# A whole filter loaded up front, weight transfers on another queue, and the last weight conversions moved into the first quads

## The chip, the cores and the metric

The kernel runs on one core of one Trainium2 chip. The metric is the device time in microseconds (us), the median of several executions. "Span" is the profiled execution from first to last instruction. It was 2769.5 us for the kernel before.

## The reference

```python
X = np.fft.rfft(x, axis=1)                      # x: (8, 3008, 256) fp32
Y = X * (filt_r + 1j * filt_i)[None, :, :]      # filter: (1505, 256), two parts
y = np.fft.irfft(Y, n=3008, axis=1)
h = y.reshape(24064, 256) @ w_in                # w_in  (256, 2048), float64 in memory
g = np.where(h > 0, h, np.exp(np.minimum(h, 0)) - 1)
out = g @ w_out                                 # w_out (2048, 256), float64 in memory
```

So there is a filter along the sequence for each of eight batches, and then a two-layer network over all tokens. The network's weights arrive as float64. The kernel reads them as pairs of 32-bit words and builds fp32 values from the bits, in 16 pieces ("weight 0" to "weight 15").

## The kernel before

Each batch is transformed in stages. Stage A multiplies chunks of x by a table (TensorE), copies the result out (ScalarE) and writes it to DRAM as z. Stage B reads z back in eight groups of frequencies, transforms each group, multiplies it by the filter (`b_unit`, four products on VectorE, two adds on GpSimd), transforms back (`bi_unit`) and writes y to DRAM. The layer then runs in quads of an up step and a down step. For batch 0 nothing of the layer can run beside stages A and B, so they are a serial prologue. Later batches' stages are spread into the layer's quads.

The prologue is what the change edits, together with a few things that hang on it:

```python
FBUFS = 3                                  # filter groups held at once
LO, HI = slice(0, 48), slice(64, 112)      # the partitions that hold filter and z

def f_read_first(g):                       # one group of the filter
    t = fbufs[g % FBUFS]
    for c, src in enumerate((filt_r, filt_i)):
        queue = nc.sync if c and g >= FBUFS else nc.gpsimd
        for a in range(2):
            r = a * 64
            k2 = 4 * g + 2 * a
            queue.dma_start(t[r:r + 24, c, :, :], raw(src, k2, [[64 * D, 24], [1, 2 * D]]))
            u = 1 if k2 == 0 else 0
            for r0, n in ((24, 16), (40, 7)):       # the mirrored half, read backwards
                queue.dma_start(t[r + r0:r + r0 + n, c, u:2, :],
                                raw(src, 64 * (r0 - 23) - k2 - u, [[64 * D, n], [-D, 2 - u], [1, D]]))
...
def w_fetch(k):                            # 512 KB of float64 weights into one of 3 places
    ...
        nc.scalar.dma_start(wd[:, ts(i, n), :].rearrange("p a w -> p (a w)"), s)

def w_convert(k):                          # VectorE: 3 tensor_scalars and 3 two-input steps,
    ...                                    # 4 adds more for odd k; ScalarE: 3 activations
    nc.scalar.activation(out=e, in_=e, func=AXT.Copy, scale=2.0 ** 23, bias=-896.0 * 2.0 ** 23)
    ...
# the prologue
for c in range(NXC):                       # stage A, six chunks
    a_unit(0, c); ...; z_write(0, c)
    w_fetch(2 + c)
    w_convert(c)
    if c == 1:
        for g in range(FBUFS):
            f_read_first(g)                # 3 of 8 groups
...
for g in range(NG + 2):                    # stage B, eight groups
    ...
        b_unit(0, g)
    ...
    if g + FBUFS < NG:
        f_read_first(g + FBUFS)
    if g < 8:
        w_fetch(8 + g)
    if g > 0:
        w_convert(6 + g)                   # a conversion in nearly every group
```

In the down step of every fourth quad stands one add on GpSimd, `nc.gpsimd.tensor_tensor(out=p3, in0=p3, in1=k[0][:, 1, 0:h], op=ALU.add)`. In quad 3 GpSimd also issues a rearrangement of the filter (`f_arrange`) for the later batches.

## Time and profile before

| | us |
|---|---|
| median of the runs of before beside the result (4 runs) | 2768.46 |
| first filter product on VectorE (end of stage A) | 55.24 |
| first matmul of the layer (end of stage B and its round trip) | 136.02 |
| first up step of quad 4 | 185.17 |
| first matmul of the next normalising step, behind the stop at 206 us | 225.92 |
| TensorE busy, of 2769.5 us | 2671.7 (96%) |

The prologue takes 136 us, 5% of the time. These five marks cut the span into pieces, and each was read from the timeline. This is how the first looks in VectorE's timeline of the kernel before (start, length, engine, line, operation, output and inputs with shapes; in brackets the idle time ahead and what ended it):

```profile
55.24 0.69 DVE L226 TENSOR_TENSOR sr<-psr,f 128x512 f32<-128x512 f32 x1 [3.00 <-PE psi L215]
```

In TensorE's waits over the whole span (waiting line, releaser, total us, times, longest), the prologue's transfers and the stop at 206 us stand out:

```profile
PE psr L215 <- DMA t<-z: 17.7, 2, 13.3
PE psn L269 <- DMA t<-yd: 13.4, 1, 13.4
PE pso L427 <- DVE g L320: 11.8, 1, 11.8
...
PE psa L171 <- DMA xc<-in_x_dram: 11.0, 3, 5.5
PE phc L315 <- DVE si L227: 5.8, 14, 0.7
```

### The profile page before, as it was taken

The numbers are of one execution on the slowest core, as the hardware profiler recorded it, in microseconds if no ns is written. First come the engines' busy times: TensorE is split into PE (matmuls) and PEld (weight loads), VectorE is DVE, ScalarE is ACT, GpSimd is POOL, SyncE is SP. The second block draws the span as 40 slices with busy tenths as digits, with TensorE's granted clock in tenths as the row PEclk, the third lists the DMA queues.
The fourth block names the chain that finished last, engine by engine and source line by source line (L and its number), as shares of the span: only waits on it lengthen the run. The fifth ranks groups of instructions, "written<-read, shape, count | busy, mean of one in ns | idle before, by whom it ended". The sixth has DMA issues, their size and how long they took to land.

```text
span 2769.5 us, 36728 instructions
## 1 busy us (share of the span) xinstructions
PE 2671.7 (96%) x13376; PEld 2282.2 (82%) x13376; DVE 1999.9 (72%) x3363; ACT 1339.6 (48%) x2297; POOL 314.1 (11%) x393
## 2 busy tenths in 40 slices
PE   4598999999999999999999999999999999999999
PEld 2197778987899878998789877898789987899887
DVE  5865877677776777767866687767777677777776
ACT  3344444544455445554455544455444544554544
POOL 4321210002000120001200021000210012000000
PEclk7599999999999999999999999999999999999999
DMA  8563321343114331243312332133321233110010
GB/s 241 159 158 97 92 63 37 101 103 94 48 39 108 89 94 37 56 119 77 82 50 76 98 84 71 37 100 98 91 57 39 78 75 94 37 39 19 22 25 16
DMA packets 144366, 214.53 MB, mean 77 GB/s; under 512 B 26368, under 2 KB 100620, under 8 KB 144186
## 3 DMA queue, kind: packets, MB, share of 16 engines
q1 hardware_dynamic: 123706, 174.57, 24.2%
q0 software_dynamic: 16160, 27.65, 4.1%
q10 hardware_dynamic: 4320, 9.96, 1.2%
q8 instruction: 106, 1.74, 0.3%
q14 instruction: 74, 0.61, 0.1%
HBM read 137.04 MB, written 78.12 MB: 78 GB/s over the span
## 4 chain that ended last, share of the span: by engine, by line
PE 85%; DVE 6%; DMA 4%; ACT 3%; issue 1%; POOL 1%; SPq 0%; DVEq 0%; ACTq 0%; POOLq 0%
PE po L388 37%; PE pha L315 11%; PE phc L315 11%; PE phd L315 11%; PE phb L315 5%; PE psa L171 3%; PE psn L269 2%; PE pso L427 2%; PE psr L215 1%; PE pva L215 1%; DVE g L320 1%; ACT e L327 1%; ACT e L326 1%; DVE c L406 1%; DVE g L331 1%
## 5 line engine op out<-in xcount | busy, mean ns | idle before, releaser
L388 PE MATMUL po<-g,wo 128*128 128x256 f32 (+1 forms) x5376 | 1324.3, 375 | 0.0
L388 PEld LDWEIGHTS po<-g,wo 128*128 128x128 f32 x5376 | 1021.4, 190 | 116.3
L326 ACT ACTIVATE e<-g 128x512 f32<-128x512 f32 (+1 forms) x576 | 357.4, 621 | 619.7 <-DVE g L320 619.5
L327 ACT ACTIVATE e<-e 128x512 f32<-128x512 f32 (+1 forms) x768 | 477.5, 622 | 24.3
L320 DVE TENSOR_TENSOR g<-phc,g 128x512 f32<-128x512 f32 (+1 forms) x384 | 259.3, 675 | 227.2 <-PE phc L315 227.2
L331 DVE SCALAR_TENSOR_TENSOR g<-e,g 128x512 f32<-128x512 f32 (+1 forms) x576 | 387.2, 672 | 14.5 <-ACT e L327 13.8
L315 PE MATMUL pha<-y,wi 128*128 128x256 f32 (+1 forms) x1536 | 395.6, 380 | 0.1
L326 ACT ACTIVATE e<-pha 128x512 f32<-128x512 f32 (+1 forms) x192 | 112.9, 588 | 530.1 <-PE pha L315 527.2
L315 PEld LDWEIGHTS pha<-y,wi 128*128 128x128 f32 x1536 | 285.0, 190 | 83.5 <-ACT t L241 34.1
L320 DVE TENSOR_TENSOR g<-phd,g 128x512 f32<-128x512 f32 (+1 forms) x384 | 261.0, 680 | 85.9 <-PE phd L315 65.7
L331 DVE SCALAR_TENSOR_TENSOR g<-e,pha 128x512 f32<-128x512 f32 (+1 forms) x192 | 129.2, 673 | 258.9 <-ACT e L327 258.9
L315 PE MATMUL phc<-ys,wi 128*128 128x256 f32 (+1 forms) x768 | 194.7, 376 | 5.8 <-DVE si L227 5.8
L395 POOL TENSOR_TENSOR k<-k,k 128x256 f32<-128x256 f32 (+1 forms) x48 | 34.5, 719 | 1457.4 <-ACT k L392 1417.9
L315 PE MATMUL phd<-y,wi 128*128 128x256 f32 (+1 forms) x768 | 194.7, 376 | 1.3
L315 PE MATMUL phc<-y,wi 128*128 128x256 f32 (+1 forms) x768 | 194.8, 376 | 0.0
L315 PE MATMUL phb<-ys,wi 128*128 128x256 f32 (+1 forms) x768 | 193.9, 375 | 0.0
L315 PE MATMUL phd<-ys,wi 128*128 128x256 f32 (+1 forms) x768 | 193.8, 375 | 0.0
L315 PEld LDWEIGHTS phc<-ys,wi 128*128 128x128 f32 x768 | 144.7, 190 | 26.8 <-issue 11.0
L315 PEld LDWEIGHTS phd<-y,wi 128*128 128x128 f32 x768 | 144.7, 190 | 22.3 <-PE phc L315 6.5
L335 ACT ACTIVATE g<-pha 128x512 f32<-128x512 f32 (+1 forms) x192 | 112.6, 586 | 103.6 <-PE pha L315 103.5
L230 POOL TENSOR_TENSOR sr<-sr,sp 128x512 f32<-128x512 f32 x64 | 81.2, 1268 | 698.3 <-DVE sp L228 698.3
L315 PEld LDWEIGHTS phb<-ys,wi 128*128 128x128 f32 x768 | 145.9, 190 | 17.0 <-issue 0.5
(92 smaller groups left out, 2939.5 us busy)
## 6 DMA issues: line engine op xcount, KB each, us to landing
z<-t SPq DMA_DIRECT2D x192, 128.0 KB
t<-z SPq DMA_DIRECT2D x128, 192.0 KB
yd<-t SPq DMA_DIRECT2D x128, 192.0 KB
t<-yd SPq DMA_DIRECT2D x192, 128.0 KB
xc<-in_x_dram SPq DMA_DIRECT2D x88, 256.0 KB
out_dram<-o SPq DMA_DIRECT2D x176, 128.0 KB
f<-fd POOLq DMA_DIRECT2D x112, 192.0 KB, 3.5
tn<-tn_t SPq DMA_DIRECT2D x48, 256.0 KB
```

What stands on the lines that cost most here:

```text
L171: nc.tensor.matmul(ps[:, u, :], w[:, r + u, :], xt[:, r + u, :], start=True, stop=True)
L215: nc.tensor.matmul(ps[:, u:u + w, :], table[k, v, :], rhs[k, u:u + w, :], start=True, stop=True)
L230: nc.gpsimd.tensor_tensor(out=sr, in0=sr, in1=p, op=ALU.subtract)
L269: nc.tensor.matmul(ps[:, ts(q, P)], t[:, i - 4 * m, ds(dh * P, P)], w[:, i - 4 * m, :], start=True, stop=True)
L315: nc.tensor.matmul(banks[key][:, a, 0:h], w_in[q][:, COMBO[n], a, :], y[n], start=start and a == 0, stop=True, skip_group_check=True)
L320: nc.vector.tensor_tensor(out=g[o], in0=i0, in1=i1, op=ALU.add)
L326: nc.scalar.activation(out=e, in_=src, func=AXT.Relu, scale=-1.0)
L327: nc.scalar.activation(out=e, in_=e, func=AXT.Exp, scale=-1.0)
L331: nc.vector.scalar_tensor_tensor(out=g[n], in0=es[n], scalar=1.0, in1=src, op0=ALU.subtract, op1=ALU.max)
L335: nc.scalar.activation(out=g["t1"], in_=mm(1, "a", True), func=AXT.Copy)
L388: nc.tensor.matmul(po[i][:, u, 0:h], w_out[q][:, COMBO[n], a, :], g[n][:, a, :], start=q == 0 and a == 0 and n in (1, 3, 6, 4), stop=True, ...
L427: nc.tensor.transpose(ps[0:w, u, ts(dh, P)], c[dh][:, ds((2 * a + u) * P, w)], eye)
```

## The change

The intent is to empty stage B. There VectorE converts a weight in almost every group, and SyncE and ScalarE queue small filter transfers and weight transfers among those of z and y. So the whole filter of batch 0 goes into one place of 32 KB per partition, which buffers of the layer take over later. The weights go to GpSimd's queue and land in the old filter buffers. Stage B keeps only every other conversion, and weights 12 to 15 are converted beside the layer's first quads. One step of each conversion goes from ScalarE to VectorE, and so does the add of the down step, from GpSimd.

```diff
-    def f_read_first(g):
+    def f_read_first(t):                   # all eight groups at once, 22 transfers
...
-                queue.dma_start(t[r:r + 24, c, :, :], raw(src, k2, [[64 * D, 24], [1, 2 * D]]))
+                nc.gpsimd.dma_start(t[r:r + 24, :, c, :, :].rearrange("q g u d -> q g (u d)"),
+                                    raw(src, 2 * a, [[64 * D, 24], [4 * D, NG], [1, 2 * D]]))
...
-                    nc.gpsimd.tensor_tensor(out=p3, in0=p3, in1=k[0][:, 1, 0:h], op=ALU.add)
+                    nc.vector.tensor_tensor(out=p3, in0=p3, in1=k[0][:, 1, 0:h], op=ALU.add)
...
-            nc.scalar.dma_start(wd[:, ts(i, n), :].rearrange("p a w -> p (a w)"), s)
+            nc.gpsimd.dma_start(wd[:, ts(i, n), :].rearrange("p a w -> p (a w)"), s)
...
-        nc.scalar.activation(out=e, in_=e, func=AXT.Copy, scale=2.0 ** 23, bias=-896.0 * 2.0 ** 23)
+        nc.vector.tensor_scalar(out=e, in0=e, scalar1=896.0, scalar2=8388608.0,
+                                op0=ALU.subtract, op1=ALU.mult)
...
+            w_fetch(2)
+            f_read_first(ff)               # ahead of weight 3 in GpSimd's queue
+            for c in range(NXC):
+                a_unit(0, c)
...
+                w_convert(c)
+                w_fetch(3 + c)
...
+                    b_unit(0, g, ff[:, g])
...
+                if g % 2 == 1:
+                    k = 6 + g // 2
+                    w_convert(k)
+                    w_fetch(k + 3)
...
+        w_convert(11)
+        w_fetch(14)
...
+        for k in range(12, 16):
+            at((0, 0, 1, 2)[k - 12], 1, w_convert, k)
```

More of the change, by code (lines that the diff above doesn't have):

```diff
@@ L125 @@
     t4p = pool("t4p", 2)
-    yp = pool("yp", 2)
-    gp = pool("gp", 2)
-    ep = pool("ep", 2)
     kp = pool("kp", 1)
-    op = pool("op", 1)
     zp = pool("zp", 2, space=DRAM)
@@ L193, in f_read @@
             nc.gpsimd.dma_start(t[r].rearrange("p c u d -> p (c u d)"), fd[g, a].rearrange("q c u d -> q (c u d)"))
-    def f_read_first(g):
-        t = fbufs[g % FBUFS]
+    def f_read_first(t):
         for c, src in enumerate((filt_r, filt_i)):
-            queue = nc.sync if c and g >= FBUFS else nc.gpsimd
             for a in range(2):
                 r = a * 64
-                k2 = 4 * g + 2 * a
-                queue.dma_start(t[r:r + 24, c, :, :], raw(src, k2, [[64 * D, 24], [1, 2 * D]]))
-                u = 1 if k2 == 0 else 0
-                for r0, n in ((24, 16), (40, 7)):
-                    queue.dma_start(t[r + r0:r + r0 + n, c, u:2, :],
-                                        raw(src, 64 * (r0 - 23) - k2 - u, [[64 * D, n], [-D, 2 - u], [1, D]]))
-            if g == 0:
-                queue.dma_start(t[24:48, c, 0, :], raw(src, 32, [[64 * D, 24], [1, D]]))
+                nc.gpsimd.dma_start(t[r:r + 24, :, c, :, :].rearrange("q g u d -> q g (u d)"),
+                                    raw(src, 2 * a, [[64 * D, 24], [4 * D, NG], [1, 2 * D]]))
+                for u in range(2):
+                    g0 = 1 if a == u == 0 else 0
+                    for r0, n in ((24, 16), (40, 7)):
+                        nc.gpsimd.dma_start(t[r + r0:r + r0 + n, g0:NG, c, u, :],
+                                            raw(src, 64 * (r0 - 23) - 4 * g0 - 2 * a - u,
+                                                [[64 * D, n], [-4 * D, NG - g0], [1, D]]))
+            nc.gpsimd.dma_start(t[24:48, 0, c, 0, :], raw(src, 32, [[64 * D, 24], [1, D]]))
     def tile_mm(ps, table, k, rhs, special):
@@ L215, in tile_mm, with b_unit @@
             nc.tensor.matmul(ps[:, u:u + w, :], table[k, v, :], rhs[k, u:u + w, :], start=True, stop=True)
-    def b_unit(b, g):
-        t, f = t2s.pop((b, g)), fbufs[(b * NG + g) % FBUFS]
+    def b_unit(b, g, f=None):
+        t = t2s.pop((b, g))
+        f = fbufs[(b * NG + g) % FBUFS] if f is None else f
         re, im = (psM.tile([P, 2, D], FP32, tag="mx", name=n) for n in ("psr", "psi"))
@@ L446, in w_fetch @@
         q, j = divmod(k, 4)
-        wd = wds[k] = gp.tile([P, 512, 2], U32, tag="g%d" % (1 + k % 3), name="wd")
+        wd = wds[k] = fbufs[k % FBUFS].bitcast(U32).rearrange("p c u d -> p (c u d)").rearrange("p (a w) -> p a w", w=2)
         if j < 2:
@@ L515 @@
     with tc.manual_schedule():
-        for c in range(XBUFS):
-            x_load(0, c, nc.scalar)
-        for f in fbufs:
-            nc.vector.memset(f, 0.0)
-        for k in range(2):
-            w_fetch(k)
-        nc.gpsimd.tensor_copy(out=junk[0:1], in_=xs[0, 1][0:1, 0, 0:1])
-        for t, d in ((gb, gb_d), (gr, gr_d), (gi, gi_d), (eye, id_d)):
-            nc.gpsimd.dma_start(t, d)
-        for c in range(NXC):
-            a_unit(0, c)
-            if c + XBUFS < NXC:
-                x_load(0, c + XBUFS, nc.scalar)
-            z_write(0, c)
-            w_fetch(2 + c)
-            w_convert(c)
-            if c == 1:
-                for g in range(FBUFS):
-                    f_read_first(g)
@@ L536 @@
-        z_read(0, 0)
-        z_read(0, 1)
-        w_convert(6)
-        for g in range(NG + 2):
-            if g >= 2:
-                bi_unit(0, g - 2)
-            if g < NG:
-                b_unit(0, g)
-                if g + 2 < NG:
-                    z_read(0, g + 2)
-            if g >= 2:
-                y_write(0, g - 2)
-            if g + FBUFS < NG:
-                f_read_first(g + FBUFS)
-            if g < 8:
-                w_fetch(8 + g)
-            if g > 0:
-                w_convert(6 + g)
+        with tc.tile_pool(name="boot", bufs=1) as bp:
+            ff = bp.tile([P, NG, 2, 2, D], FP32, name="ff")
+            for k in range(2):
+                w_fetch(k)
+            for c in range(XBUFS):
+                x_load(0, c, nc.scalar)
+            nc.vector.memset(ff, 0.0)
+            nc.gpsimd.tensor_copy(out=junk[0:1], in_=xs[0, 2][0:1, 0, 0:1])
+            for t, d in ((gb, gb_d), (gr, gr_d), (gi, gi_d)):
+                nc.gpsimd.dma_start(t, d)
+            w_fetch(2)
+            f_read_first(ff)
+            for c in range(NXC):
+                a_unit(0, c)
+                if c + XBUFS < NXC:
+                    x_load(0, c + XBUFS, nc.scalar)
+                z_write(0, c)
+                w_convert(c)
+                w_fetch(3 + c)
+            z_read(0, 0)
+            z_read(0, 1)
+            for g in range(NG + 2):
+                if g >= 2:
+                    bi_unit(0, g - 2)
+                if g < NG:
+                    b_unit(0, g, ff[:, g])
+                    if g + 2 < NG:
+                        z_read(0, g + 2)
+                if g >= 2:
+                    y_write(0, g - 2)
+                if g % 2 == 1:
+                    k = 6 + g // 2
+                    w_convert(k)
+                    w_fetch(k + 3)
@@ L554 @@
+        yp = pool("yp", 2)
+        gp = pool("gp", 2)
+        ep = pool("ep", 2)
+        op = pool("op", 1)
         y_read(0, 0)
+        w_convert(11)
+        w_fetch(14)
+        nc.scalar.dma_start(eye, id_d)
         n_unit(0, 0)
@@ L567 @@
             at(c - 1, 0, x_load, 1, c)
+        for k in range(12, 16):
+            at((0, 0, 1, 2)[k - 12], 1, w_convert, k)
+        at(0, 1, w_fetch, 15)
         at(3, 1, f_arrange)
+        for f in fbufs:
+            at(4, 1, nc.vector.memset, f, 0.0)
         for b in range(B):
```

## The prediction

> **What bounds the kernel now.** I first read the page's busy shares and the 40 slices of 69 us.
>
> ```profile
> PE   4598999999999999999999999999999999999999
> PEclk7599999999999999999999999999999999999999
> ```
>
> TensorE is full from the fourth slice on; only the first three have room. In a table of stretches of the same trace, 240 to 2700 us held 2452.9 us of TensorE work in 2460. The change can gain or lose only in the first 240 us and on what keeps TensorE fed later. So I cut those 240 us where the trace changes character (columns: stretch and length, busy us and count of TensorE, weight loads, VectorE, ScalarE, GpSimd, granted clock, DMA share, GB/s).
>
> ```profile
> 0.00:51.90 51.90, 17.88 (x48) 12.20 (x49) 29.11 (x57) 20.49 (x35) 23.56 (x48) 0.78 0.96 268
> 51.90:122.40 70.50, 45.69 (x136) 11.49 (x136) 57.00 (x85) 19.43 (x34) 37.59 (x47) 0.50 0.57 159
> 122.40:136.00 13.60, 0.18 (x2) 0.01 (x1) 11.05 (x23) 5.45 (x10) 0.00 (x0) 0.50 0.53 149
> ...
> 206.00:218.00 12.00, 0.17 (x1) 0.00 (x0) 1.63 (x5) 0.00 (x0) 8.52 (x10) 0.66 0.46 83
> 218.00:223.40 5.40, 5.38 (x17) 4.59 (x18) 3.14 (x5) 3.19 (x7) 0.00 (x0) 0.50 0.25 63
> ```
>
> Stage A (to 51.9, first batch's first transform) has its DMA engines 96% busy: it is bound by transfers. Stage B (51.9 to 122.4, filter product and inverse) has VectorE 81% busy. From 122.4 to 136.0 TensorE waits for a round trip through DRAM while VectorE still converts weights; the layer begins at 136.0. At 206 TensorE stops for 12 us in the layer's fifth quad (one quad is one up step and one down step, about 12.5 us), and then runs 5.4 us at half clock. The timeline of VectorE and of GpSimd shows why:
>
> ```profile
> 202.11 0.38 DVE L406 TENSOR_TENSOR k<-k,c 128x224 f32<-128x224 f32 x1
> 216.37 0.39 DVE L406 TENSOR_TENSOR c<-c,k 128x224 f32<-128x224 f32 x1 [13.88 <-POOL k L395]
> ```
>
> ```profile
> 209.01 3.27 POOL L505 DMA_DIRECT2D fd<-in_filt_i_dram  x2
> ...
> 215.10 0.52 POOL L513 DMA_DIRECT2D fd<-in_filt_i_dram  x1 [1.75 <-DMA fd<-in_filt_i_dram]
> 215.69 0.65 POOL L395 TENSOR_TENSOR k<-k,k 128x224 f32<-128x224 f32 x1
> ```
>
> A 0.65 us add of the down step stands on GpSimd behind the issues of the filter's rearrangement (fd), and VectorE waits 13.88 us for it. Last, in SyncE's waits up to 140 us, transfers of x, z and f wait for weight transfers:
>
> ```profile
> SPq L206 <- DMA wd<-in_moe_w_in_dram: 11.6, 2, 6.0
> SPq L187 <- DMA wd<-in_moe_w_in_dram: 7.2, 2, 6.7
> SPq L183 <- DMA wd<-in_moe_w_in_dram: 4.9, 2, 4.5
> ```
>
> [...] L187 is the read of z for the second group; it makes the second group's matmuls start at 59.6 instead of about 55.
>
> [...] the conversion's two tensor_scalars on weights take 0.42 us each in stage A, but 1.12 and 1.49 beside GpSimd's add and subtract in stage B.
>
> **The change, part by part.**
>
> *Stage A, +4.6 us.* The whole filter (2 x 1505 rows of 1 KB, 3.1 MB) must land before the second stage instead of 1.1 MB. Needed by then: x 3.1, tables 1.6, z 3.1, filter 3.1, weights 0 to 5 3.1 MB, in all 14.0 MB. The old stage moved 51.9 x 268 = 13.9 MB, so bandwidth alone gives about 52 us again. But GpSimd issues weight 3 after the 22 filter transfers, and the built program makes each of its issues wait for the eighth one before it. I estimate that weight 3 lands near 43 us. Its two ScalarE conversions stand in front of the evacuation of the fifth chunk, so chunks five and six and their writes of z finish about 3 us late. VectorE then has conversions 3, 4 and 5 (5.6, 3.9, 5.6 us at stage A durations) before the first filter product, which gives another 1.5. Second stage starts effectively at 56.5. The memset of 8192 elements (8 x 0.91 = 7.3 us) ends before VectorE's first weight arrived in the old trace (12.3).
>
> *Stage B to the layer's first matmul, -21.5 us.* Old: 51.9 to 136.0, 84.1 us. VectorE is the chain there: 4 products at 0.62 pitch, 2.5 us per group, and a conversion in nearly every group, 5.5 us, or 7.3 with the four adds (read at 72.3 to 80.4 and 65.0 to 72.3). The new one has conversions 6 to 9 between products (10 and 11 lie behind the last product). ScalarE's exponent step goes to VectorE (+0.46) and takes its round trip (0.7) away: still 5.4 and 7.2. Two groups now cost 2.5 + 5.4 (or 7.2) + 2.5 + 2.2, the last term being the exposed matmuls of the odd group at half clock (74.8 to 77.0). From the stage's start: first products end at 5.9, second at 9.1 (the late z read is gone), conversion 6 at 14.5, products 17.0 and 21.7, conversion 7 28.9, products 31.4 and 36.1, conversion 8 41.5, products 44.0 and 48.7. After that the old tail: GpSimd 2.2, inverse 2.4, evacuation 1.1, issue 0.3, then 7.9 us from evacuation to first layer matmul (128.1 to 136.0), 13.9 in all: 62.6 us. Conversions 9, 10 and 11 (7.2 + 3.9 + 5.6) fill 16.7 of the time after the last product, and the layer needs VectorE at 16.5: no loss.
>
> *First quads, +14 us.* Conversions 12 and 13 stand on VectorE after the tail of quad 0 and before quad 1's first add: 3.7 + 5.6 = 9.3 us. There is no slack for them: in the old trace VectorE finished that tail at 153.2, while TensorE had been in quad 1 since 148.0, and its add at 154.18 ended 0.1 us before the matmul that overwrites that bank (154.94). ScalarE's first copy of quad 1 stands behind conversion 13 too. TensorE stops after four steps of quad 1, and restarts at half clock: 10 us. Conversion 14 (3.7) and 15 (5.6) fall in quads where VectorE idled 1.7 and 2.4 us at a time and another chunk's transform comes before the critical matmul: 1.5 and 2. Three memsets of 0.91 in quad 4: 0.5.
>
> *The stop at 206, -14.5 us.* The add goes to VectorE, where it costs 0.38 us 48 times, in an engine that is 72% busy. The stop of 11.8 us and half of the 5.4 us at half clock go. The rearrangement itself keeps its place; its first reader comes in quad 7, so it stays hidden.
>
> Sum: 4.6 - 21.5 + 14 - 14.5 = -17.4, so 2751 us.
>
> **Rivals.** (a) *The conversions in the quads are absorbed:* VectorE's 72% speaks for it, the 0.1 us between add and matmul against. Then about 2738. (b) *The filter and weights starve each other in stage A:* the 0.96 DMA share and the eight-deep GpSimd queue speak for it[...]. GpSimd's filter issues in the old stage A mostly keep 0.5 us beside such conversions, which speaks against. If stage A ends near 66, about 2761. (c) *TensorE becomes the bound of stage B:* it already works 45.7 of 70.5 us at half clock and its work does not shrink. My cycle needs about 6 us of it per group of 7 on average, so this is close: then stage B gains 4 us less, 2755[...].
>
> **Range and chances.** The terms are good to about 5, 5, 5 and 2 us, in quadrature some 9; with 80% that is 2738 to 2765. A change of 2% is 55 us. All of stage B's excess and the stop together are not that large once the transfers of stage A stay, and no loss I can see reaches 55: 0.98 for within 2%.
>
> **What would show it.** First filter product near 60 us and last before 110; the first layer matmul near 119; a TensorE hole of 6 to 10 us in quad 1 with VectorE on conversion lines; no hole at the c add of quad 4; TensorE full afterwards. The prediction is wrong if stage A passes 62, if the hole in quad 1 is missing, or if a new stop appears when the rearranged filter is first read.

The marked cuts took out what no trace of this case shows. No term of the sum was in them: it came to 4.6 - 21.5 + 14 - 14.5 = -17.4 us, so 2751 us. One reason of rival (b) and the second branch of rival (c) are among the cuts.

## The result, and the profile after

The changed kernel takes 2763.14 us (median of 4 runs, 2761.57 to 2766.57) against 2768.46 us for before (4 runs, 2767.99 to 2768.98). The ratio is 0.9982, with a 95% interval of 0.9965 to 1.0. A ratio here is the mean time of one kernel's fast runs over that of the other's of the same rounds, so it is not quite the ratio of the medians. The time lies in the predicted range and within 2%. But the forecast was a gain of 17 us, and 5 came.

The five marks say where the time went:

| piece | before | after | difference | predicted |
|---|---|---|---|---|
| start to first filter product (stage A) | 55.24 | 74.79 | +19.6 | +4.6 |
| to the layer's first matmul (stage B) | 80.78 | 56.35 | -24.4 | -21.5 |
| to quad 4 (first quads) | 49.15 | 61.95 | +12.8 | +14 |
| to the next normalising step (the stop) | 40.75 | 27.79 | -13.0 | -14.5 |
| to the end | 2543.58 | 2540.82 | -2.8 | 0 |
| span | 2769.5 | 2761.7 | -7.8 | -17.4 |

(The spans are of one execution each, so their difference is not quite that of the medians.) One row of the table is badly off, the first.

The page of the changed kernel shows, in 40 slices of 69 us, that the first slice lost TensorE work and that the second and third gained it:

```profile
PE   2689999999999999999999999999999999999998
PEclk7599999999999999999999999999999999999999
```

The table of stretches of the changed kernel (columns as in the prediction) shows a stage A that is now 74.8 us long, with DMA engines as full as before and fewer bytes moved per second:

```profile
0.00:20.00 20.00, 8.64 (x25) 5.78 (x26) 12.67 (x14) 6.80 (x11) 6.00 (x15) 1.00 0.95 236
20.00:40.00 20.00, 3.79 (x16) 2.71 (x16) 6.58 (x14) 2.29 (x4) 8.02 (x15) 0.74 1.08 227
40.00:60.00 20.00, 3.75 (x8) 2.52 (x8) 5.10 (x11) 2.82 (x5) 6.82 (x13) 0.50 0.94 222
...
74.80:131.10 56.30, 32.32 (x123) 9.57 (x116) 51.51 (x85) 14.96 (x27) 25.79 (x26) 0.59 0.60 167
```

The kernel before moved 303 GB/s between 20 and 40 us at a share of 1.05. From 20 to 60 us the compute engines of the changed kernel do little: VectorE is busy for 11.7 of 40 us. Stage B is the row from 74.8: VectorE is 91% busy, and that stretch is short, as intended.

What they wait for is in the timelines. GpSimd issues weight 3 only at 46.98, after the 22 filter transfers. Its issues also waited for landings: the one at 23.26 waited 2.60 us for the eighth before it (gb), and those at 25.23 and 27.93 waited 0.23 and 2.15 us for the eighth before each (weight 2):

```profile
46.98 1.14 POOL L452 DMA_DIRECT2D f<-in_moe_w_out_dram  x2
```

ScalarE waits 21 us for it, with the copy of chunk 5 behind its two conversion steps:

```profile
54.67 0.67 ACT L471 ACTIVATE wl<-f 128x512 f32<-128x512 uint32 x1 [21.16 <-DMA f<-in_moe_w_out_dram]
55.25 0.61 ACT L472 ACTIVATE wf<-wm 128x512 f32<-128x512 uint32 x1
55.77 0.57 ACT L168 ACTIVATE t<-psa 128x512 f32<-128x512 f32 x1
```

From there the chain runs on: the copy of chunk 6 at 61.0, its z written by 68.3, the first group read by 72.8, and the first product on VectorE, which answers to the 55.24 of before:

```profile
74.79 0.69 DVE L223 TENSOR_TENSOR sr<-psr,ff 128x512 f32<-128x512 f32 x1 [5.65 <-PE psi L211]
```

TensorE's waits after, for the same lines as before:

```profile
PE psa L167 <- DMA xc<-in_x_dram: 28.8, 6, 16.3
PE psr L211 <- DMA t<-z: 24.1, 1, 24.1
PE psn L266 <- DMA t<-yd: 11.4, 1, 11.4
PE pha L312 <- ACT g L332: 8.6, 3, 7.1
...
PE phc L312 <- DVE si L224: 2.6, 14, 0.2
...
PE pso L424 <- DVE g L317: 1.2, 1, 1.2
```

The wait for x grew most, from 11.0 to 28.8 us: the two reads of x issued after 19 us landed in 12.7 us (median), against 4.1 without the filter (the run below). It does not end last in stage A, though. The chain of work that ended last, followed back from the end of the trace, leads through the filter's transfers, weight 3 and the copy of chunk 6. The stop of 11.8 us at the pso line has become 1.2, and the recurring phc wait has halved. A new line stands among them: pha waits for ScalarE, once for 7.1 us. That is the hole in quad 1, after which TensorE runs at about half clock (a granted 0.57 from 153.3 to 160.1 us, with 1.86 us for four matmuls that take 0.92 later):

```profile
153.31 1.86 PE L312 MATMUL pha<-y,wi 128*128 128x224 f32 x4 [7.05 <-ACT g L332]
...
160.09 0.92 PE L312 MATMUL phc<-y,wi 128*128 128x224 f32 x4
```

VectorE's timeline of quad 4 has the moved add (L392, 0.39 us) on VectorE now, and the later add that needs its result (c<-c,k), which waited 13.88 us for GpSimd before, waits for nothing:

```profile
202.56 0.39 DVE L392 TENSOR_TENSOR k<-k,k 128x224 f32<-128x224 f32 x1 [1.79 <-ACT k L389]
...
210.45 0.39 DVE L403 TENSOR_TENSOR c<-c,k 128x224 f32<-128x224 f32 x1
```

### The profile page after: what moved, and what is told of

It is laid out like the page before. It is cut to its first block, busy times and chain, and to the rows that moved or that the text cites. A ratio compares the mean times of both kernels' runs of the same rounds, so it can differ in the third digit from the quotient of the medians.

```text
span 2761.7 us, 36465 instructions
## 1 busy us (share of the span) xinstructions
PE 2661.4 (96%) x13376; PEld 2281.0 (83%) x13376; DVE 2021.7 (73%) x3428; ACT 1331.3 (48%) x2281; POOL 268.4 (10%) x322
## 4 chain that ended last, share of the span: by engine, by line
PE 86%; DVE 7%; ACT 3%; DMA 2%; issue 2%; POOL 0%; SPq 0%; DVEq 0%; ACTq 0%; POOLq 0%
PE po L385 37%; PE pha L312 11%; PE phc L312 11%; PE phd L312 11%; PE phb L312 5%; PE psa L167 3%; PE psn L266 2%; PE pva L211 2%; PE psr L211 2%; PE pso L424 2%; DVE g L317 1%; ACT e L323 1%; ACT e L324 1%; DVE c L403 1%; DVE g L328 1%
## 5 line engine op out<-in xcount | busy, mean ns | idle before, releaser
L324 ACT ACTIVATE e<-e 128x512 f32<-128x512 f32 (+1 forms) x768 | 477.6, 622 | 24.4
L328 DVE SCALAR_TENSOR_TENSOR g<-e,g 128x512 f32<-128x512 f32 (+1 forms) x576 | 387.4, 673 | 11.6 <-ACT e L324 11.1
L312 PEld LDWEIGHTS phd<-ys,wi 128*128 128x128 f32 x768 | 145.8, 190 | 16.5
```

Of the source, the lines that this page charges most:

```text
L312: nc.tensor.matmul(banks[key][:, a, 0:h], w_in[q][:, COMBO[n], a, :], y[n], start=start and a == 0, stop=True, skip_group_check=True)
L324: nc.scalar.activation(out=e, in_=e, func=AXT.Exp, scale=-1.0)
L328: nc.vector.scalar_tensor_tensor(out=g[n], in0=es[n], scalar=1.0, in1=src, op0=ALU.subtract, op1=ALU.max)
```

## The experiments

The theory I formed on the result: the filter's transfers take far more of the DMA engines than their bytes, so stage A is longer by about what they take. The rivals: it is the order in GpSimd's queue (weight 3 behind 22 transfers); it is the conversions that stand before the evacuations (the copies out of TensorE's results); or it is a property of the source in DRAM. "Product" below means the start of VectorE's first filter product, 74.79 us in the changed kernel. It is read from one trace of each run: kernels with the same stage A gave 74.5 to 75.0 (four traces), but 60.8 and 62.7 in another pair, so less than 2 us says little. Diffs are against the changed kernel unless said otherwise. "Engine-us per MB" is the share of the 16 engines that a queue's packets took, times 16, times the stretch, over the MB moved. GpSimd's queue (q0) carries the weights as well as the filter, so its row is a mixture.

### How much does the filter cost? No filter

The result is wrong, since the filter stays zero.

```diff
-            f_read_first(ff)
```

> The changed kernel without the first batch's 22 filter transfers (the place keeps its zeros, so the result is wrong on purpose). Theory Q (the filter stands in front of weight 3 on GpSimd's queue, and weight 3 stands in front of ScalarE's evacuations): weight 3 lands near 25 us instead of 54.7, the first filter product starts near 52 instead of 74.8, the time falls by about 20 us to some 2743. Rival S (stage A is long because of the conversions and the memset on VectorE[...], the filter's bytes do not matter): the first product stays above 68, time within 5 us of 2763.

Measured: 2740.24 us (2 runs; ratio 0.9895, 0.9875 to 0.9915), product at 51.82, and the stretch from 20 to 40 us moves 321 GB/s:

```profile
20.00:40.00 20.00, 8.20 (x28) 5.87 (x27) 16.37 (x34) 9.38 (x17) 3.61 (x7) 0.74 1.02 321
```

The filter's transfers cost all 23 us, from 51.8 to 74.8. At the 268 GB/s of the old stage A, 3.1 MB would be 11.6.

### Is it the order in the queue? Weights 3 and 4 first

```diff
-            f_read_first(ff)
...
                 w_convert(c)
                 w_fetch(3 + c)
+                if c == 1:
+                    f_read_first(ff)
```

> Same transfers, other order on GpSimd's queue: weights 3 and 4 are issued before the filter, weight 5 still after it. Theory Q: the fifth and sixth chunk are evacuated near 41 to 46 us instead of 56 and 61; the first product then waits only for the filter and conversion 5, near 64; about 9 us faster than the changed kernel, some 2754. Rival B (plain bandwidth: the DMA engines are full, so order only shifts who waits): first product stays at 72 or later, 2761 or more.

Measured: 2761.35 us (4 runs; ratio 0.9971, 0.9956 to 0.9986), product at 71.90. It missed the 2754 expected if the order were the cause. Weight 3 now reaches ScalarE at 30.74, but ScalarE's next copy waits 18 us for writes of z instead:

```profile
50.16 1.08 ACT L168 ACTIVATE t<-psa 128x512 f32<-128x512 f32 x2 [18.24 <-DMA z<-t]
```

What came behind the filter's transfers became the wait here: the writes of z, 18.24 us, where it had been weight 3, 21.16 us. With weights 3 and 4 first, the order decides who waits, and only about 3 us of the length.

### Is it the conversions? Weights 3 to 10 in stage B

```diff
-                w_convert(c)
-                w_fetch(3 + c)
+                if c < 3:
+                    w_convert(c)
+                    w_fetch(3 + c)
...
-                if g % 2 == 1:
-                    k = 6 + g // 2
-                    w_convert(k)
-                    w_fetch(k + 3)
+                if g < 8:
+                    w_convert(3 + g)
+                    w_fetch(6 + g)
```

> Conversions 3 to 5 are taken out of stage A (ScalarE no longer stands behind weight 3 there) and stand in stage B, one conversion per group. Theory Q: the first product starts near 60 instead of 74.8, but stage B, bound by VectorE, takes three conversions more (5.4 to 7.2 us each, 17 in all), so the layer's first matmul stays within 4 us of 131 and the time within 4 us of 2763. Rival B: the first product stays at 70 or later and the time rises by 10 or more.

Measured: 2777.57 us (4 runs; ratio 1.0031, 1.0014 to 1.0047), 14 us more than expected. The product came at 64.47, ten us earlier, although the copy of chunk 5 still waited 12.8 us for writes of z. But stage B then took 80.0 us instead of 56.4 (layer's first matmul at 144.44). Three more conversions on the engine that bounds stage B, and one in each of the eight groups, cost more than the wait that they had filled. I had put too little on that. The ten us do show that the conversions in front of the first product are a part of stage A's length.

### Smaller pieces: the filter in two halves between the weights

```diff
-    def f_read_first(t):
+    def f_read_first(t, lo, hi):           # groups lo to hi - 1
...
                 w_fetch(3 + c)
+                if c in (0, 2):
+                    f_read_first(ff, 2 * c, 2 * c + 4)
```

> The filter in two halves of four groups: weight 3, half one, weights 4 and 5, half two (44 smaller transfers, same bytes). Theory Q: weights 3 to 5 land early enough that VectorE converts them in stage A; first product near 60, layer's first matmul near 117, time near 2750. Rival B: as long as all bytes share the same engines, first product no earlier than 70, time 2760 or more.

Measured: 2754.11 us (4 runs; ratio 0.9943, 0.9928 to 0.9958), product at 60.80. The stretch from 20 to 40 us moves 307 GB/s, that from 40 to 60 only 192. So the second half meets the stage's end rather than its middle. The product comes 14.0 us earlier, of which 9.0 are left in the time. GpSimd's queue from 19 to 40 us and from 40 to 62 (packets, MB, share of 16 engines):

```profile
q0 software_dynamic: 1240, 2.72, 41.2%
...
q0 software_dynamic: 1120, 2.59, 62.6%
```

That is 51 and 85 engine-us per MB. The first half was not dear, although it goes to the same few partitions as the second.

### The first quads: four conversions ahead of the layer

```diff
         w_convert(11)
         w_fetch(14)
+        w_convert(12)
+        w_fetch(15)
+        for k in range(13, 16):
+            w_convert(k)
...
-        for k in range(12, 16):
-            at((0, 0, 1, 2)[k - 12], 1, w_convert, k)
-        at(0, 1, w_fetch, 15)
```

> Conversions 12 to 15 undone from the quads: they run behind conversion 11, before the layer. Theory H (the hole of 7 us and the half clock after it come from conversions 12 and 13 standing in front of quad 1's copy and add): no TensorE idle stretch in quads 1 to 3, first layer matmul to the start of quad 4 about 49 us as in the kernel before instead of 62.1, but the layer's first combination waits 15 us or so longer for VectorE; total 2763 to 2768. Rival K (the slow first quads come from the filter place being handed over, or from cold operands): the hole stays and the time rises by 15.

Measured: 2767.87 us (2 runs; ratio 0.9996, 0.9976 to 1.0016). The hole in quad 1 is gone, but pha waits 10.0 us for the layer's input, because VectorE converts first. Quad 4 starts 64.6 us after the layer's first matmul, against 62.0 in the changed kernel. The conversions have to be paid somewhere, and in front of the layer they are paid in full.

### The first quads: one conversion in the middle of each

```diff
-            at((0, 0, 1, 2)[k - 12], 1, w_convert, k)
-        at(0, 1, w_fetch, 15)
+            at(k - 12, 0, w_convert, k)
+        at(0, 0, w_fetch, 15)
```

> Conversions 12 to 15 one per quad, in the middle of quads 0 to 3 (behind the up step's seventh bank) instead of two at the end of quad 0. Theory H: VectorE's burst is then at most 5.6 us and TensorE still has 5 to 6 us of work that needs none of it; the quads lose 2 to 5 us instead of 13: about 2754. If what counts is VectorE's total work in the quads, not where it stands, they still lose 10 or more: 2760 or more.

Measured: 2755.83 us (4 runs; ratio 0.9952, 0.9937 to 0.9967). Quad 4 starts 53.1 us after the layer's first matmul instead of 62.0, and TensorE's wait in the quads shrinks from 8.6 to:

```profile
PE pha L312 <- ACT g L332: 1.8, 3, 0.9
```

So 9 of the 12.8 us lost in the first quads were the place of the conversions. Two of them back to back between quads 0 and 1 made the hole and the half clock after it: without that, pha waits at most 1.21 us in the quads, and the four matmuls after that wait take 1.02 us instead of 1.86.

### The stop at 206 us: only the add back on GpSimd

```diff
-                    nc.vector.tensor_tensor(out=p3, in0=p3, in1=k[0][:, 1, 0:h], op=ALU.add)
+                    nc.gpsimd.tensor_tensor(out=p3, in0=p3, in1=k[0][:, 1, 0:h], op=ALU.add)
```

> Only the add of the down step goes back to GpSimd. Theory: the stop in quad 4 comes back, 12 us idle and half of 5 us at half clock, so +13 to +15, about 2777; and if the 3 us that the rest of the kernel gained belong to the same line, TensorE's waits on phc go back from 2.6 to 5.8 us and the time to 2780. Rival: the stop was owed to the old stage B and does not come back (2763).

Measured: 2779.23 us (4 runs; ratio 1.0034, 1.0019 to 1.0049), 16 us more. In TensorE's waits both lines come back to what they were before:

```profile
PE pso L424 <- DVE g L317: 10.7, 1, 10.7
...
PE phc L312 <- DVE si L224: 5.7, 14, 0.5
```

The one line of code is worth 16 us: the stop, and some 3 us of small waits that the prediction did not have, which are the -2.8 us in the table's last piece. (Between the two traces 11.9 us lie at the stop, 3.7 behind it, and 2.0 in stage B, which the line does not touch.) Why the add on GpSimd lengthens the small waits is not shown.

### Halves and mid-quad conversions together

Both edits above at once, the correct result.

> The filter in halves and the conversions in mid quad together. If the two are independent, the gains add: 2754 (halves, measured) less what the mid-quad kernel gains over 2763; about 2745. If the layer's first quads then meet the late weight transfers (weights 12 to 15 land too late), 2750 or more.

Measured: 2747.84 us (4 runs; ratio 0.9923, 0.9906 to 0.994). Product at 62.66, quad 4 at 176.77. The gains of 9.0 and 7.3 us add up nearly, to 15.3.

### Why are the filter's bytes dear? A pitch of 63 KB

From one partition's rows to the next the filter's source steps 64 KB. That this step makes the bytes dear was a guess, which no earlier run shows. Here every 64 rows became 63, which reads wrong rows. (For the rates in the expectation: the changed kernel moved 174 GB/s from 28 to 37 us in the mean, at a share of 1.07.)

```diff
-                [[64 * D, 24], [4 * D, NG], [1, 2 * D]]
+                [[63 * D, 24], [4 * D, NG], [1, 2 * D]]
...                                                       # likewise in the mirrored half
```

> Why do the filter's transfers keep all DMA engines busy and move only 90 to 160 GB/s (0.96 to 1.0 share, 28 to 37 us)? The filter is read here with 63 rows (63 KB) in place of 64 rows (64 KB) between one partition's data and the next; sizes, partitions, order and queue are the same, only the rows read are other ones (a wrong result on purpose). Theory P: [...]then the filter moves at 250 GB/s or more, the first filter product comes at 62 us or before and the time falls to 2752 or less. Rival S: it is the short rows or the few partitions; then the rate at 28 to 37 us stays below 180 GB/s, the product stays at 72 to 76 and the time at 2759 to 2766.

Measured: 2764.11 us (2 runs; ratio 0.9981, 0.9961 to 1.0001), product at 75.97. The pitch is not the cause.

### Forward rows only, 23 partitions

```diff
+            for h in range(4):
+                for s in range(4):
+                    nc.gpsimd.dma_start(t[23 * s:23 * s + 23, 2 * h:2 * h + 2, c, :, :].rearrange("q g u d -> q g (u d)"),
+                                        raw(src, 16 * h + 2 * s, [[64 * D, 23], [8 * D, 2], [1, 2 * D]]))
```

(in place of all the filter's transfers; wrong result)

> The same number of bytes of filter within 4% (3.0 MB), the same 64 KB between partitions, but read forward only, as 2 KB rows, in 32 transfers of 23 partitions and 94 KB each, so no row of 1 KB and no transfer of 7 partitions is left (a wrong result on purpose). If the short rows and the narrow transfers are what is dear, the first filter product comes at 64 us or before. If the pitch or the count of partitions is, it stays at 71 to 77 us, and the rate while the filter moves stays below 180 GB/s.

Measured: 2780.21 us (2 runs; ratio 1.0039, 1.0019 to 1.006), product at 88.78, outside of both expectations. This run settles nothing about rows, because it brought a trouble of its own. In its table of transfers from 19 to 60 us most packets are under 512 B, although every row has 2 KB:

```profile
DMA packets 15056, 6.71 MB, mean 164 GB/s; under 512 B 11461, under 2 KB 14013, under 8 KB 15056
```

The issues also took GpSimd about 1.1 us each (16 in 17.45 us from 41.6 on), where the changed kernel's take 0.55. The sizes in the packed trace say more. 11040 packets of GpSimd's queue, up to 75 us, have 8 bytes: 345, or 15 x 23, for each of the 32 transfers. From these counts I estimate that one DMA engine carried all rows of such a transfer and the other 15 got a tiny packet for each. That is not tested. The packets with data were not slow: see the control below.

### Thirds

On top of the halves-and-mid-quad form:

```diff
-                if c in (0, 2):
-                    f_read_first(ff, 2 * c, 2 * c + 4)
+                if c in (0, 1, 3):
+                    f_read_first(ff, *((0, 2), (2, 4), None, (4, 8))[c])
```

> The best form so far (halves of the filter between weight fetches, one conversion in each of the quads 0 to 3) with the filter in three parts: groups 0 and 1 after the fetch of weight 3, 2 and 3 after weight 4, 4 to 7 after weight 6. If each part's bytes ahead of a weight are what delays it, weight 4 reaches its conversion 3 to 5 us earlier than with halves (46.2 us there), the first product moves from 62 to about 58 us and the time from 2747.8 to about 2744. If the issues on GpSimd[...] are the limit, the product comes no earlier, GpSimd's first subtract of stage B waits behind them, and the time is 2748 to 2754.

Measured: 2753.92 us (4 runs; ratio 0.9947, 0.993 to 0.9963), worse than halves. Weight 4 did come earlier (41.85), but the last 22 issues ran on GpSimd until 71, and stage B's first subtract stood behind them:

```profile
PE pva L212 <- POOL sr L228: 15.8, 1, 15.8
```

So GpSimd's own work stood behind its issues again, as in the old stop at 206 us (13.88 us), in a new place.

### Is it the narrow destination? The same bytes to 96 partitions

Each of the filter's transfers goes to 24, 16 or 7 partitions. That so few of them make the bytes dear was my guess (theory W below), which no run before this one shows. So, with a wrong result:

```diff
+            for h in range(4):
+                nc.gpsimd.dma_start(t[0:96, 2 * h:2 * h + 2, c, :, :].rearrange("q g u d -> q g (u d)"),
+                                    raw(src, 20 * h, [[15 * D, 96], [10 * D, 2], [1, 2 * D]]))
```

(in place of all the filter's transfers)

> As many bytes of filter as in the changed kernel (3.1 MB), at the same place of the same queue and as rows of 2 KB, but each transfer goes to 96 partitions instead of 24, 16 or 7 (8 transfers of 393 KB; a wrong result on purpose). Theory W (the narrow destination is what is slow[...]): the filter then costs what weights and z cost, 50 to 56 engine-us per MB[...]; the rate at 28 to 37 us is 250 GB/s or more, the first filter product comes at 60 to 66 us and the time is 2747 to 2755. Rival (it is the filter's bytes or the queue, whatever the partitions): product at 71 to 77, time 2759 to 2766.

Measured: 2751.34 us (2 runs; ratio 0.9935, 0.9915 to 0.9955), product at 62.22. Weight 3 reaches ScalarE 13.6 us earlier than in the changed kernel:

```profile
41.09 0.69 ACT L461 ACTIVATE wl<-f 128x512 f32<-128x512 uint32 x1 [11.01 <-DMA f<-in_moe_w_out_dram]
```

The queues' table of this run, from 19 to 54 us (packets, MB, share of 16 engines; q0 carries what GpSimd issues):

```profile
q0 software_dynamic: 1920, 6.49, 58.4%
```

That is 0.584 x 16 x 35 / 6.49 = 50 engine-us per MB. The changed kernel's same row gives 72:

```profile
q0 software_dynamic: 1868, 4.52, 58.0%
```

### The control: the same eight transfers to 24 partitions

The 96-partition form also had fewer transfers and no rows of 1 KB. Against it, only the destination changes (wrong as well):

```diff
-            for h in range(4):
-                nc.gpsimd.dma_start(t[0:96, 2 * h:2 * h + 2, c, :, :].rearrange("q g u d -> q g (u d)"),
-                                    raw(src, 20 * h, [[15 * D, 96], [10 * D, 2], [1, 2 * D]]))
+            for h, r in enumerate((0, 24, 64, 88)):
+                nc.gpsimd.dma_start(t[r:r + 24, :, c, :, :].rearrange("q g u d -> q g (u d)"),
+                                    raw(src, 360 * h, [[15 * D, 24], [10 * D, NG], [1, 2 * D]]))
```

> The control for e12_wide: the same 8 transfers of 393 KB, of the same rows of 2 KB of the same source, at the same place of the queue; only the destination differs, 24 partitions with all eight groups instead of 96 partitions with two (a wrong result on purpose). Theory W (the width is what is slow): the first filter product is back at 70 us or later, the engines pay 70 or more engine-us per MB on GpSimd's queue, and the time is 2758 or more. If the fewer, larger transfers or the absence of 1 KB rows made e12_wide fast: product at 60 to 66, 50 to 56 engine-us per MB, time 2748 to 2755.

Measured: 2760.14 us (2 runs; ratio 0.9967, 0.9938 to 0.9996), product at 71.41, and in the same stretch:

```profile
q0 software_dynamic: 1856, 5.44, 69.2%
```

That is 71 engine-us per MB. The same rows in the same number of transfers cost 50 into 96 partitions and 71 into 24, and the product moves by 9.2 us. So, with the whole filter sent in a row, the width of the destination is the cause. (The two runs are of different chips, with two executions each; their medians lie 8.8 us apart and the two executions of each within 1 us, while the intervals of the ratios just overlap.) The remaining 3.4 us between this run and the changed kernel (74.79) go with the 22 transfers and the shorter rows together, which no run separates.

Writes of z, which are unchanged, landed in 12.1 us (median, from 19 to 54 us) beside the narrow filter, whole or in the eight-transfer control, and in 5.9 beside the wide one.

How the width acts is not shown. It may be the number of DMA engines that share a transfer: the control has 32 packets of 8 bytes for each of its transfers (4 x 8; from this I estimate that 4 of 16 engines got no rows), the wide form has none. No run tests it. The median packet of 4 KB on GpSimd's queue from 21 to 42 us took 301 ns in the control, 201 in the wide form, and 168 in the form with 23 partitions above, which is as narrow as the control. So narrow bytes are not dear by themselves, as the first of the two halves (51) showed too. In the kernel before, the small filter transfers share GpSimd's queue with three tables only, and from 13 to 43 us that queue cost 59:

```profile
q0 software_dynamic: 1244, 1.33, 16.3%
```

What the runs show to be dear is a long row of transfers to 24 partitions and fewer, with the engines full: 71 engine-us per MB at shares of 1.07 and 1.02 (20 to 40 and 40 to 60 us).

### The two halves of the partitions by turns

The filter's rows go to two halves of the partitions, from 0 and from 64. On the guess that transfers to both halves at once would be cheaper, those of the two halves, which the changed kernel issues five of the one and then five of the other, were issued by turns, the correct result:

```diff
-                for u in range(2):             # inside the loop over the halves
...
+            for u in range(2):
+                for r0, n in ((24, 16), (40, 7)):
+                    for a in range(2):         # one half, the other half, by turns
```

> Correct result. The changed kernel with one thing altered: the transfers to partitions 0 to 46 and to 64 to 110 are issued by turns instead of eleven or twelve of the one half and then those of the other. Theory W: [...]the product comes 4 to 8 us earlier (67 to 71) and the time falls to 2755 to 2759. If the eight under way already cover both halves, or the width is not the cause, product 72 to 76 and 2760 to 2765.

Measured: 2760.95 us (4 runs; ratio 0.9971, 0.9954 to 0.9988), product at 72.64. That is 2 us, not the 4 to 8 expected, and the interval overlaps that of the changed kernel. For the whole filter, the order of halves is not shown to matter. (The expectation counts eleven or twelve transfers of one half in a row; the code has five, so eight under way, the depth at which its issues waited in the trace above, already reached both halves.)

### The best version

The same order in the halves-and-mid-quad form, correct result:

> Correct result. The best form so far (halves of the filter between weight fetches and one conversion in each of the quads 0 to 3, 2747.8 us) with the two halves of the partitions by turns, as in the other run. Theory W: each half of the filter costs some 2 to 3 us less, product at 58 to 60 instead of 62.7, time 2743 to 2746. If the order of the partitions does nothing: 2746 to 2750.

Measured: 2743.29 us (4 runs, 2742.63 to 2744.51; ratio 0.9906, 0.9891 to 0.9921). This beats both kernels, by 27 us against the 2770.24 of before in its call. VectorE's first product:

```profile
57.95 0.69 DVE L226 TENSOR_TENSOR sr<-psr,ff 128x512 f32<-128x512 f32 x1 [6.02 <-PE psi L214]
```

It came at 62.66 without the turns. These are single traces, two traces of the stage A without turns differ by 1.9 us, and the intervals of the two ratios overlap, so the further 4 us are likely rather than proved.

## Why the prediction was right or wrong

**Stage A: wrong, and it is the step that failed.** The step was "so bandwidth alone gives about 52 us again", with its consequence "I estimate that weight 3 lands near 43 us". Both priced the filter's bytes like any others, at the old stage's 268 GB/s. In place of that the runs showed DMA engines that were as full but moved only 227 and 222 GB/s from 20 to 60 us, with weight 3 in use at 54.7. That delay of 11.7 us is most of the 15.0 by which the first product came too late. Sent in a row, bytes into 24 partitions cost 71 engine-us per MB on GpSimd's queue, and the same bytes into 96 cost 50. With the wide destination the product came at 62.2 and weight 3 was used at 41.1, which is nearly what the prediction had for the real one (59.8 and 43). So the rest of the step's working held, and one term was mis-sized: without the filter the product comes 23 us earlier, where its bytes alone give 11.6. How the width makes it so is not shown. Rival (b) named starvation between filter and weights and had stage A end near 66. The direction was right and the size was not. Of its reasons, the full DMA engines held (shares of 0.95, 1.08 and 0.94 in the three stretches up to 60 us). The eight-deep queue was not tested by itself: weights 3 and 4 first gained 3 us, the halves between the weights 14.

**Stage B: right.** The saving was 24.4 for 21.5, so 56.35 us against 59.3. (The 62.6 of the working begin some 3 us before the first product. The working once puts conversion 9 between the products, but its sum, like the code, has it behind the last.) The prediction's rival (c) expected TensorE to bind. Instead the granted clock was higher (0.59 in the mean of this stretch, 0.50 before), for a reason that is not shown.

**First quads: right.** +12.8 for +14, with the hole in quad 1 where it was expected. The run with one conversion in the middle of each quad got 9 of it back, so the cause is the place of the conversions. The run with them ahead of the layer shows that moving them out of the quads gains nothing. Rival (a), that the quads absorb them, falls for this place; in mid quad all but 4 us are absorbed.

**The stop: right.** -13.0 for -14.5. Undoing that one line cost 16 us.

**To the end: missed.** -2.8 for nothing. The add on VectorE also shortens a wait that recurs 14 times, from 5.8 to 2.6 us in all. It went back to 5.7 when the add did.

**The sum.** The pieces miss by +15.0, -2.9, -1.2, +1.5 and -2.8 us. That the time still fell into the range, with its first step wrong, is the luck of a wide range and of misses that partly cancel.

**What would make it wrong.** The prediction said it would be wrong if stage A passed 62 us. It passed that by 13.

## What to carry to other kernels

Do not price a transfer by its bytes alone where the DMA engines are full and many transfers to few partitions follow one another: read their engine time per MB beside that of wide ones (here 71 and 50). A trace in which they are few is not enough: in the kernel before they cost 59, and in a row 71. Try work on an engine at its limit in small pieces, in places where another engine's work bridges it: here one conversion in the middle of each quad took 2755.83 us against 2763.14 with two back to back, and halves of the filter between the weights 2754.11 against the same 2763.14 with all of it ahead of them. Look for short operations behind an engine's transfer issues: on GpSimd here such an add held others up for 13.88 us, and such a subtract for 15.8.
